# Rest rows masked by the overflow flag, and the last expert's writes behind the overflow branch

## The chip, the cores and the metric

The kernel runs on one core of one Trainium2 chip. The metric is the time of one execution on the device in microseconds (us); the median of three runs is given with the least and the greatest.

## What is computed

An attention layer in chunks of 32 queries (4 batches, 8 heads, 768 positions, 64 wide) gives x, 3072 rows of 512. A mixture of 8 experts follows: each row goes to the two experts with the greatest noisy logits, and the output row is the weighted sum of what they return.

```python
noisy_logits = logits + noise_scale * noise
top2 = np.argpartition(-noisy_logits, 2, axis=1)[:, :2]
top2_l = np.take_along_axis(noisy_logits, top2, axis=1)
top2_l = top2_l - top2_l.max(-1, keepdims=True)
top2_w = np.exp(top2_l)
top2_w /= top2_w.sum(-1, keepdims=True) + 1e-09
out = np.zeros((N, D), dtype=np.float32)
for e in range(E):
    for k in range(2):
        mask = top2[:, k] == e
        h = np.maximum(x[mask] @ w1[e], 0.0)
        out[mask] += top2_w[mask, k, None] * (h @ w2[e])
```

## The kernel before

**Stages.** The attention and the gate come first; their lists of rows are ready some 130 us into the span. The experts follow, one after the other, and fill the rest. The change lies in this second part.

**Rows by pairs of experts.** There are 28 pairs of experts. Each pair has a tile of up to MT = 96 rows that both of its experts work on. Expert e has three pairs for which it is the first (out_of(e)) and three for which it is the second (in_of(e)); four more pairs (numbered from QP = 24) join e and e + 4. Rows of a pair beyond 96 are *rest rows*: up to RU = 64 a pair and RS = 160 an expert are collected in an expert's rest list, in two blocks, A (96 rows) and B (64 rows, written in half rows). If a pair or an expert has still more, the kernel counts that in flag, and a branch at the very end runs overflow(), which works the rows over 96 of every pair off again, in tiles of 128. The flag is copied as a whole number to nxt.

**One expert.** mm1 computes the hidden layer (TensorE, PE), with relu on ScalarE (ACT) and VectorE (DVE). mm2_tiles computes three output tiles. For the first expert of a pair the result is scaled into a new tile y; for the second it is added to that y (line 1063), which is then complete and is noted in the list later. Each PSUM tile holds 32 more rows of another kind, copied to the tile unit: the rest rows of block A (ins_) or the rows of the four pairs from QP (outs). For experts 4 to 7 finish_q scales yq, which holds the other expert's share, and adds unit to it (lines 1085 and 1086); yq goes to later too.

**Writes.** put writes the rows of a y to their places in out, by an indirect DMA that GpSimd (POOL) issues (line 943); places out of bounds are left out. flush issues all that later holds. put_rest (line 960) does the same for a rest tile. A rest row has two experts in different rest lists, so the second expert first reads what the first wrote: get_prev (line 969) reads pA and pB from out after clear_prev has cleared them on ACT (line 1124), and ins_ adds them. Reads of this kind wait for earlier rest writes; writes of y are declared free of both.

**Places of rest rows.** rest_decode (called three times, for experts 0 and 1, 2 and 3, 4 to 7) computes a place from the table entry t: t - 128, or a large number where t is 0, so that unused slots are out of bounds (lines 1250 and 1251).

**Order.** The order on every engine is written out by hand: the loop of lines 1443 to 1482, an iteration an expert. For e below 7 an iteration ends with finish_q, flush, ins_(e). For e = 7 it is: the hidden layer, clear_prev, flush, get_prev, ins_(7), flush, outs(7), finish_q(7). So before the change the three y and the two rest tiles of ins_(7) are written inside the loop, and the three y of outs(7) and the last yq stay in later. A second block then loads nxt on every engine, on DVE behind the last write to yq (last), branches, and flushes (lines 1487 to 1492):

```python
        with tc.issue_after(last[0].ins):
            nov = nc.values_load(nxt[0:1, 0:1], min_val=0, max_val=E * (E + 1),
                                 skip_runtime_bounds_check_because="a count of the counts that are too large")
        with tc.If(nov > 0):
            overflow()
        flush()
```

Line 1518 is the end of the program, where all engines wait for each other.

Of the kernel before, what the change touches and what calls it, by code (L numbers as in the profile page):

```python
# [2 lines left out]

# [8 lines left out]
F32 = mybir.dt.float32  # L12
# [3 lines left out]
Alu = mybir.AluOpType  # L16
# [6 lines left out]
def kernel(  # L23
# [14 lines left out]
    nc = tc.nc  # L38
# [6 lines left out]
    N = B * S  # L45
    Dm = H * D
    E, F = moe_w1.shape[0], moe_w1.shape[2]
# [45 lines left out]
    QP = 3 * E  # L93
    MT = 96
# [3 lines left out]
    BIG = 65536  # L98
# [843 lines left out]
    def put(y, ix, rows=None, n=N):  # L942
        i = nc.gpsimd.indirect_dma_start(  # L943
            out=out if rows is None else rows, out_offset=bass.IndirectOffsetOnAxis(ap=ix, axis=0), in_=y, in_offset=None,
            bounds_check=n - 1, oob_is_err=False)
        for g in ("put", "prev", "rest"):
            tc.declare_no_dep(i.ins, group=g, reason=apart)
        pin(i)
        tc.add_to_no_dep_group("put", i.ins)
# [100 lines left out]
    def mm2_tiles(e, ps, h, unit):  # L1050
        for k, g in enumerate(ps):
            p = psY.tile([128, Dm], F32, name="p_y")
            for f in range(FB):
                nc.tensor.matmul(out=p, lhsT=h[:, f, k, :], rhs=w2(e, f), start=(f == 0), stop=(f == FB - 1))  # L1054
            x = pairs[g].index(e)
            wt = wl[0:MT, x, g:g + 1]
            if x == 0:
                y = ys[g] = yp.tile([128, Dm], F32, name="y")
                nc.scalar.activation(out=y[0:MT], in_=p[0:MT], func=Act.Copy, scale=wt)  # L1059
                keep_unit(0, unit[32 * k:32 * k + 32], p)  # L1060
            else:
                y = ys.pop(g)
                nc.vector.scalar_tensor_tensor(out=y[0:MT], in0=p[0:MT], scalar=wt, in1=y[0:MT], op0=Alu.mult, op1=Alu.add)  # L1063
                keep_unit(1, unit[32 * k:32 * k + 32], p)
                later.append((y[0:MT], dst[0:MT, g:g + 1]))

    def flush():
        for y, ix in later:
            put(y, ix)
        later.clear()  # L1070

    def outs(e):
# [4 lines left out]
        else:  # L1077
            yr_of[e] = unit

    def finish_q(e):  # L1080
        if e >= 4:
            unit = yr_of.pop(e)
            q = QP + e - 4
            y = yq.pop(e - 4)[0:MT]
            nc.vector.tensor_scalar(out=y, in0=y, scalar1=wl[0:MT, 0, q:q + 1], scalar2=None, op0=Alu.mult)
            last[0] = nc.vector.scalar_tensor_tensor(out=y, in0=unit[0:MT], scalar=wl[0:MT, 1, q:q + 1], in1=y, op0=Alu.mult, op1=Alu.add)
            later.append((y, dst[0:MT, q:q + 1]))

    prev = {}
    yr_of = {}  # L1090
# [3 lines left out]
    def ins_(e):  # L1094
        wA, wB, dA, dB, hA, hB_ = rest_of[e]
        pA, pB = prev.pop(e) if e else (None, None)

        def rest_tile():
            p = psY.tile([128, Dm], F32, name="p_y")[:, 0:Dm // 2]
            for f in range(FB):  # L1100
                for g in range(2):
                    nc.tensor.matmul(out=p[g * RU:(g + 1) * RU], lhsT=hB[:, f, :], rhs=w2(e, f, g * Dm // 2, Dm // 2),  # L1102
                                     start=(f == 0), stop=(f == FB - 1), tile_position=(0, g * RU))
            yB = yrp.tile([128, Dm // 2], F32, name="yB", bufs=1)
            if e == 0:
                nc.vector.tensor_scalar(out=yB, in0=p, scalar1=wB, scalar2=None, op0=Alu.mult)
            else:
                nc.vector.scalar_tensor_tensor(out=yB, in0=p, scalar=wB, in1=pB, op0=Alu.mult, op1=Alu.add)  # L1108
            return yB

        unit = yrp.tile([128, Dm], F32, name="yr")
        mm2_tiles(e, in_of(e), hI, unit)
        put_rest(rest_tile(), dB, outB, 2 * N)
        if e == 0:
            nc.vector.tensor_scalar(out=unit[0:MT], in0=unit[0:MT], scalar1=wA, scalar2=None, op0=Alu.mult)
        else:
            nc.vector.scalar_tensor_tensor(out=unit[0:MT], in0=unit[0:MT], scalar=wA, in1=pA[0:MT], op0=Alu.mult, op1=Alu.add)
        put_rest(unit[0:MT], dA, out, N)

    def clear_prev(e):  # L1120
        pA = yrp.tile([128, Dm], F32, name="pA", bufs=1)
# [33 lines left out]
    adr = late.tile([128, 2, E], I32, name="adr")  # L1155
    early = late.tile([128, 2, E], F32, name="early")
    nxt = late.tile([128, 1], I32, name="nxt")
    tsb = late.tile([RU, NP, 8], F32, name="tsb")
    oh_at = scol[0] + 4096
    oh_t = wflat[:, oh_at:oh_at + NG * RU].rearrange("p (g t) -> p g t", g=NG)  # L1160
# [10 lines left out]
    def rest_tables(p, part):  # L1171
        if part == 0:
            pm = p.rearrange("p (a b) -> p a b", a=E)
            nc.vector.tensor_scalar(out=cnt2, in0=pm, scalar1=-float(MT), scalar2=0.0, op0=Alu.add, op1=Alu.max)
            return
        over = late.tile([128, E, E + 1], F32, name="over")
        nc.vector.tensor_scalar(out=over[:, :, 0:E], in0=cnt2, scalar1=float(RU), scalar2=None, op0=Alu.is_gt)
        nc.vector.tensor_scalar(out=cnt2, in0=cnt2, scalar1=float(RU), scalar2=None, op0=Alu.min)
        nc.vector.scalar_tensor_tensor(out=wadr, in0=cnt2, scalar=-float(NP), in1=dadr, op0=Alu.mult, op1=Alu.add)
        cur = cnt2  # L1180
        for i in range(3):
            k = 1 << i
            o = inc2[i % 2]
            nc.vector.tensor_copy(o[:, :, 0:k], cur[:, :, 0:k])
            nc.vector.tensor_tensor(out=o[:, :, k:E], in0=cur[:, :, k:E], in1=cur[:, :, 0:E - k], op=Alu.add)
            cur = o
        ge = late.tile([128, 2, E, E], F32, name="ge")
        for b in range(2):
            nc.vector.tensor_scalar(out=ge[:, b], in0=cur, scalar1=rslot[:, b:b + 1], scalar2=None, op0=Alu.is_le)
        nc.vector.tensor_tensor(out=ge, in0=ge, in1=wadr.unsqueeze(1).to_broadcast([128, 2, E, E]), op=Alu.mult)  # L1190
        red = late.tile([128, 2, E], F32, name="red2")
        nc.vector.tensor_reduce(out=red, in_=ge, axis=AX, op=Alu.add)
        nc.vector.tensor_tensor(out=adr, in0=red, in1=radr, op=Alu.add)
        for b in range(2):
            nc.vector.tensor_scalar(out=early[:, b], in0=cur.rearrange("p a b -> p (a b)")[:, 0:E * E:E + 1],
                                    scalar1=rslot[:, b:b + 1], scalar2=None, op0=Alu.is_gt)
        nc.vector.tensor_scalar(out=over[:, :, E:E + 1], in0=cur[:, :, E - 1:E], scalar1=float(RS), scalar2=None, op0=Alu.is_gt)
        flag = late.tile([128, 1], F32, name="flag")
        nc.vector.tensor_reduce(out=flag, in_=over.rearrange("p a b -> p (a b)"), axis=AX, op=Alu.add)
        nc.vector.tensor_copy(nxt, flag)  # L1200

    def rest_onehots():
        t1 = late.tile([128, NG], F32, name="t1")
# [27 lines left out]
    def rest_decode(lo, hi):  # L1231
# [16 lines left out]
        nc.vector.tensor_tensor(out=w[:, 0], in0=d, in1=w[:, 1], op=Alu.subtract)  # L1248
        nc.scalar.activation(out=w, in_=w, func=Act.Exp)
        nc.vector.tensor_scalar(out=u, in0=t, scalar1=0.0, scalar2=float(BIG), op0=Alu.is_equal, op1=Alu.mult)  # L1250
        nc.vector.scalar_tensor_tensor(out=t, in0=t, scalar=-128.0, in1=u, op0=Alu.add, op1=Alu.max)
        nc.vector.scalar_tensor_tensor(out=t[:, 1], in0=t[:, 1], scalar=2.0, in1=half.to_broadcast([128, m]), op0=Alu.mult, op1=Alu.add)
        nc.vector.tensor_copy(d_, t)
        nc.vector.tensor_scalar(out=u, in0=ea, scalar1=-float(BIG), scalar2=float(BIG), op0=Alu.mult, op1=Alu.add)
# [134 lines left out]
    with tc.manual_schedule(engines={ET.PE, ET.Activation, ET.DVE, ET.SP, ET.Pool}):  # L1389
# [53 lines left out]
        for e in range(1, E):  # L1443
            n = e + 1
            if n == E:
                mm1_rest(e, q=False, engs=(0,))
            mm1_main(e, in_of(e), hI)
            clear_prev(e)
            if e in (1, 3):
                dx = rest_decode(n, 4 if e == 1 else E)  # L1450
                for _ in range(3):
                    next(dx)
            new = gathers(in_of(e + 2)) + gathers(out_of(e + 2)) if e + 2 < E else []
            if e + 2 < 4:
                gather_main(QP + e + 2)
            if n < E:
                rest_rows(n)
            flush()
            get_prev(e)
            load_next()  # L1460
            if n == E:
                ins_(e)
                flush()
            outs(e)
            if n < E:
                turn_rest(n)
            turns(new)
            if e + 2 < E:
                turn_q(e + 2)
            if n < E:  # L1470
                mm1_rest(e, q=False, engs=(0,))
                mm1_main(n, out_of(n), hO)
                mm1_rest(n, r=False)
            finish_q(e)
            if n < E:
                flush()
            if e == 1:
                for k in range(4, E):
                    rest_facts(k)
            load_next()  # L1480
            if n < E:
                ins_(e)
# [40 lines left out]
```

## Time and profile before

| what | us |
|---|---|
| median of 3 runs (least to greatest) | 346.47 (346.16 to 347.88) |
| the profiled execution | 349.4 |
| its span, first to last instruction | 347.8 |
| PE busy in the span | 278.9 (80%) |
| POOL busy in the span | 203.4 (58%) |
| DVE busy in the span | 183.6 (53%) |
| ACT busy in the span | 155.0 (45%) |

Rows of a timeline or a group give the source line, the engine, the operation, the tile written and the tiles read. A name such as POOLq is the sequencer of an engine: it loads registers, branches and handles semaphores, and can be ahead of its engine. "Idle before" with an arrow names what ended the wait. PEclk is the share of TensorE's full clock that was granted. A POOL row of a DMA covers its issue only; the data lands later.

### The profile page before, as it was taken

Reading aid. Unit: us, or ns where it says so; the run is one execution under the profiler, and the core shown is the slowest. Engines: PE = TensorE matmul, PEld = TensorE weight load, DVE = VectorE, ACT = ScalarE, POOL = GpSimd, SP = SyncE. Lnnn points to the kernel's source line nnn. Section 1 sums busy time; section 2 is a strip of 40 time slices with the busy share of each in tenths; the row PEclk is TensorE's granted clock in tenths of the full one; section 3 lists DMA queues with packets and bytes.
Section 4 is the critical chain, followed back from the end, with each engine's and each line's share of the span. In section 5 each row is a group of like instructions: output and inputs, shape, how many; then the busy total and the mean of one; then the engine's idle time right before and its main releaser. Section 6 shows DMA issues by size and latency. Waiting matters only on the chain.

```text
span 347.8 us, 9190 instructions
## 1 busy us (share of the span) xinstructions
PE 278.9 (80%) x3746; PEld 207.2 (60%) x3762; DVE 183.6 (53%) x406; ACT 155.0 (45%) x320; POOL 203.4 (58%) x291
## 2 busy tenths in 40 slices
PE   0678788766777746797999999999999999999800
PEld 0557677655667636656668766676676666866300
DVE  4675568676499677236363533644345354353500
ACT  4657638553565312534445363553443534534200
POOL 4669679982046247745777776571745735626531
PEclk9978899998899556999999999999999999999955
DMA  7999969999516512421686996999999699504221
GB/s 127 211 211 179 224 111 210 192 168 161 106 28 107 140 31 59 109 59 47 114 119 139 160 127 158 185 217 166 186 150 198 159 170 157 152 25 118 79 77 45
DMA packets 43277, 46.78 MB, mean 135 GB/s; under 512 B 20241, under 2 KB 33621, under 8 KB 43228
## 3 DMA queue, kind: packets, MB, share of 16 engines
q0 software_dynamic: 22800, 38.26, 58.8%
q1 hardware_dynamic: 19884, 7.83, 11.6%
q8 instruction: 31, 0.51, 0.6%
q14 instruction: 18, 0.15, 0.1%
q10 hardware_dynamic: 544, 0.03, 0.1%
HBM read 59.11 MB, written 11.33 MB: 203 GB/s over the span
## 4 chain that ended last, share of the span: by engine, by line
PE 44%; issue 6%; DMA 5%; DVE 4%; POOL 2%; ACT 2%; POOLq 1%; DVEq 0%; ACTq 0%
PE p_h L992 23%; PE p_y L1054 17%; DMA pB<-out_dram,ri 4%; POOL out_dram L943 2%; PE p_y L1102 2%; ACT w_all L1149 1%; DMA xt<-xd,main_src 1%; ACT w_all L980 1%; PE p_xt L1214 1%; DVE yq L1048 0%; POOLq L1518 0%; PE p_x L623 0%; POOL out_dram L960 0%; PE p_xt L1148 0%; PE p_list L372 0%
## 5 line engine op out<-in xcount | busy, mean ns | idle before, releaser
L992 PE MATMUL p_h<-w_all 128*128 128x288 bf16 (+3 forms) x1120 | 96.1, 248 | 4.0 <-ACT w_all L1149 2.8
L992 PEld LDWEIGHTS <-w_all 128*128 128x128 bf16 x1120 | 83.1, 99 | 17.7 <-issue 5.9
L1054 PE MATMUL p_y<-w_all 128*128 128x512 bf16 x368 | 83.6, 379 | 1.7 <-ACT yr L1048 0.5
L980 ACT ACTIVATE w_all<-p_h 128x288 bf16<-128x288 f32 (+3 forms) x137 | 46.8, 375 | 51.8 <-PE p_h L992 50.3
L1054 PEld LDWEIGHTS <-w_all 128*128 128x128 bf16 x384 | 37.0, 98 | 43.3 <-issue 1.8
L412 POOL COPY w_all<-w_all 128x512 bf16<-128x512 bf16 (+1 forms) x59 | 42.0, 781 | 13.0 <-PE p_t L432 8.4
L978 DVE TENSOR_SCALAR w_all<-p_h 128x288 bf16<-128x288 f32 (+1 forms) x65 | 30.7, 476 | 35.5 <-PE p_h L992 34.0
L938 POOL DMA_INDIRECT xt<-xd,main_src x28 | 27.0, 963 | 10.1 <-issue 7.3
L1063 DVE SCALAR_TENSOR_TENSOR y<-p_y,main_w,y 96x512 f32<-96x512 f32 x24 | 17.9, 747 | 24.8 <-PE p_y L1054 24.8
L943 POOL DMA_INDIRECT out_dram<-y,main_dst x24 | 22.5, 936 | 12.6 <-issue 6.1
L1048 ACT COPY yr<-p_y 32x512 f32<-32x512 f32 x24 | 13.9, 579 | 35.6 <-DVE y L1063 34.5
L960 POOL DMA_INDIRECT out_dram<-yB,rd x8 | 9.8, 1226 | 28.6 <-DVE yB L1108 28.0
L1059 ACT ACTIVATE y<-p_y,main_w 96x512 f32<-96x512 f32 x24 | 16.4, 682 | 21.2 <-PE p_y L1054 20.1
L432 PE MATMUL p_t<-identf,w_all 128*128 128x128 f32 x120 | 20.6, 314 | 1.3 <-ACT pT L587 0.8
L938 POOL DMA_INDIRECT xt<-xd,rs x16 | 14.8, 924 | 11.3 <-DVE rw L1246 6.3
L1048 DVE COPY yr<-p_y 32x512 f32<-32x512 f32 x12 | 8.3, 694 | 22.3 <-ACT y L1059 21.3
L614 DVE TENSOR_TENSOR w_all<-ps_o,rs 128x512 bf16<-128x512 f32 x24 | 15.7, 683 | 6.5 <-PE ps_o L601 5.6
L1223 POOL DMA_INDIRECT fr<-tdr,adr x16 | 16.1, 1007 | 4.9 <-issue 4.9
L461 PE MATMUL p_v<-identf,w_all 128*128 128x128 f32 x96 | 15.9, 305 | 2.7 <-ACT w_all L436 1.8
L432 PEld LDWEIGHTS p_t<-identf,w_all 128*128 128x128 f32 x120 | 15.9, 163 | 2.7 <-POOL w_all L412 1.4
L587 ACT COPY pT<-p_p 128x1024 bf16<-128x1024 bf16 x11 | 11.1, 1012 | 12.7 <-PE p_p L581 12.4
L501 DVE TENSOR_REDUCE mx<-ps_s 128x16 f32<-128x1024 f32 x12 | 14.7, 1223 | 2.8 <-PE ps_s L488 2.5
(231 smaller groups left out, 405.2 us busy)
## 6 DMA issues: line engine op xcount, KB each, us to landing
w_all<-in_moe_w_dram POOLq DMA_DIRECT2D x16, 1024.0 KB
w_all<-in_k_dram POOLq DMA_DIRECT2D x4, 768.0 KB
w_all<-in_q_dram POOLq DMA_DIRECT2D x4, 768.0 KB
w_all<-in_v_dram POOLq DMA_DIRECT2D x4, 768.0 KB
xd<-w_all SPq DMA_DIRECT2D x24, 128.0 KB
w_all<-mvn SPq DMA_DIRECT2D x24, 32.0 KB
w_all<-xt SPq DMA_TRANSPOSE x39
xt<-xd,main_src POOLq DMA_INDIRECT x28
```

Source lines behind the costliest of these rows:

```text
L412: i = eng.tensor_copy(to, x)
L432: nc.tensor.transpose(out=p_t[:, s, :], in_=m.bitcast(F32)[:, s * 128:(s + 1) * 128], identity=identf)
L938: pin(nc.gpsimd.indirect_dma_start(out=t[0:n].bitcast(I32), out_offset=None, in_=src_, in_offset=bass.IndirectOffsetOnAxis(ap=ix, axis=0)))
L943: i = nc.gpsimd.indirect_dma_start(out=out if rows is None else rows, out_offset=bass.IndirectOffsetOnAxis(ap=ix, axis=0), in_=y, in_offse ...
L978: nc.vector.tensor_scalar(out=out_, in0=in_, scalar1=0.0, scalar2=None, op0=Alu.max)
L980: nc.scalar.activation(out=out_, in_=in_, func=Act.Relu)
L992: nc.tensor.matmul(out=o if len(xk.shape) == 2 else o.rearrange("p (j t) -> p j t", j=xk.shape[1]), lhsT=w_all[:, e % WR, kp * F + f * 128 ...
L1048: (nc.scalar.copy if eng else nc.vector.tensor_copy)(to, p[MT:128, :])
L1054: nc.tensor.matmul(out=p, lhsT=h[:, f, k, :], rhs=w2(e, f), start=(f == 0), stop=(f == FB - 1))
L1059: nc.scalar.activation(out=y[0:MT], in_=p[0:MT], func=Act.Copy, scale=wt)
L1063: nc.vector.scalar_tensor_tensor(out=y[0:MT], in0=p[0:MT], scalar=wt, in1=y[0:MT], op0=Alu.mult, op1=Alu.add)
L1223: i = nc.gpsimd.indirect_dma_start(out=fr[0:n, b, e], out_offset=None, in_=tdr, in_offset=bass.IndirectOffsetOnAxis(ap=adr[0:n, b, e:e + 1 ...
```

## The change

- rest_tables makes a column away = 65536 x flag - 128, and rest_decode uses it in place of the constant -128. With a flag of 0 the places are the same; with a flag above 0 every rest row is out of bounds, and overflow() alone writes rows over 96.
- The puts of expert 7 are all kept in later until behind the branch: three y of ins_, the rest tiles yB and yr, three y of outs, yq. later now holds calls, and the flush behind ins_(7) is gone.
- In ins_(6) a flush stands ahead of the rest tile, so its three y are put ahead of the two rest tiles instead of an iteration later.
- The scaling of yq is taken out of finish_q into scale_q, which stands ahead of outs(e).

```diff
@@ flush, finish_q
-                later.append((y[0:MT], dst[0:MT, g:g + 1]))
+                later.append(partial(put, y[0:MT], dst[0:MT, g:g + 1]))
 
     def flush():
-        for y, ix in later:
-            put(y, ix)
+        for f in later:
+            f()
         later.clear()
...
+    def scale_q(e):
+        if e >= 4:
+            q = QP + e - 4
+            y = yq[e - 4][0:MT]
+            nc.vector.tensor_scalar(out=y, in0=y, scalar1=wl[0:MT, 0, q:q + 1], scalar2=None, op0=Alu.mult)
+
     def finish_q(e):
...
-            nc.vector.tensor_scalar(out=y, in0=y, scalar1=wl[0:MT, 0, q:q + 1], scalar2=None, op0=Alu.mult)
             last[0] = nc.vector.scalar_tensor_tensor(out=y, in0=unit[0:MT], scalar=wl[0:MT, 1, q:q + 1], in1=y, op0=Alu.mult, op1=Alu.add)
-            later.append((y, dst[0:MT, q:q + 1]))
+            later.append(partial(put, y, dst[0:MT, q:q + 1]))
@@ ins_
         mm2_tiles(e, in_of(e), hI, unit)
-        put_rest(rest_tile(), dB, outB, 2 * N)
+        if e == E - 2:
+            flush()
+        yB = rest_tile()
+        later_rest = [partial(put_rest, yB, dB, outB, 2 * N), partial(put_rest, unit[0:MT], dA, out, N)]
+        if e < E - 1:
+            later_rest.pop(0)()
...
-        put_rest(unit[0:MT], dA, out, N)
+        if e < E - 1:
+            later_rest.pop(0)()
+        later.extend(later_rest)
@@ rest_tables, rest_decode
+    away = late.tile([128, 1], F32, name="away")
...
         nc.vector.tensor_copy(nxt, flag)
+        nc.vector.tensor_scalar(out=away, in0=flag, scalar1=float(BIG), scalar2=-128.0, op0=Alu.mult, op1=Alu.add)
...
-        nc.vector.scalar_tensor_tensor(out=t, in0=t, scalar=-128.0, in1=u, op0=Alu.add, op1=Alu.max)
+        nc.vector.scalar_tensor_tensor(out=t, in0=t, scalar=away, in1=u, op0=Alu.add, op1=Alu.max)
@@ the loop
             if n == E:
                 ins_(e)
-                flush()
+            scale_q(e)
             outs(e)
```

More of the change, by code (lines that the diff above doesn't have):

```diff
@@ L1 @@
 import math
+from functools import partial
 from contextlib import ExitStack
```

## The prediction

> **What bounds the kernel now.** I read the page's row of slices first: where does PE stop, and what runs after it?
>
> ```profile
> PE   0678788766777746797999999999999999999800
> POOL 4669679982046247745777776571745735626531
> DMA  7999969999516512421686996999999699504221
> ```
>
> A slice is 347.8 / 40 = 8.7 us. PE is full up to the 37th slice and has nothing in the last two. So there are two stages: a long one that PE sets, and a tail of some 17 us in which POOL (it issues the indirect DMAs that write the output) and the DMA are alone. The change acts mainly on the tail. The timeline of POOL shows its order:
>
> ```profile
> 318.45 0.99 POOL L969 DMA_INDIRECT pA<-out_dram,ri  x1 [0.51 <-ACT pA L1124]
> 319.75 1.03 POOL L969 DMA_INDIRECT pB<-out_dram,ri  x1 [0.30 <-issue]
> ...
> 324.21 1.27 POOL L960 DMA_INDIRECT out_dram<-yB,rd  x1 [3.42 <-DVE yB L1108]
> ...
> 325.78 0.95 POOL L960 DMA_INDIRECT out_dram<-yr,rd  x1 [0.30 <-issue]
> ...
> 327.04 0.92 POOL L943 DMA_INDIRECT out_dram<-y,main_dst  x1 [0.30 <-issue]
> ...
> 328.26 0.92 POOL L943 DMA_INDIRECT out_dram<-y,main_dst  x1 [0.30 <-issue]
> ...
> 329.49 1.00 POOL L943 DMA_INDIRECT out_dram<-y,main_dst  x1 [0.30 <-issue]
> ...
> 335.41 0.92 POOL L943 DMA_INDIRECT out_dram<-y,main_dst  x1 [4.92 <-DVEq L1490]
> ...
> 339.08 0.92 POOL L943 DMA_INDIRECT out_dram<-yq,main_dst  x1 [0.30 <-issue]
> ```
>
> Five puts of expert 7 (yB, yr, three y) are issued by 330.5. POOL then does nothing for 4.92 us, and issues four more from 335.41 to 339.08, (339.08 - 335.41) / 3 = 1.22 us apart. The hole is the overflow branch. The instructions of the branch lines, by the view of one source line (duration least/median/most, then first and last start), say what the hole is made of:
>
> ```profile
> L1488 POOLq TENSOR_LOAD <-nxt x1: 507/507/507, 326.6 to 326.6; - x1
> L1490 POOLq COMPARE_BRANCH  x1: 58/58/58, 327.2 to 327.2; - x1
> L1490 POOLq EVENT_SEMAPHORE  x6: 17/30/43, 329.9 to 332.6; - x6
> L1490 POOLq INC_SWDGE_SEM  x1: 1795/1795/1795, 332.7 to 332.7; - x1
> L1490 PEldq COMPARE_BRANCH  x1: 3782/3782/3782, 328.1 to 328.1; - x1
> L1490 DVEq COMPARE_BRANCH  x1: 72/72/72, 331.6 to 331.6; - x1
> L1490 DVEq EVENT_SEMAPHORE  x1: 21/21/21, 334.5 to 334.5; - x1
> L1518 POOLq DRAIN  x3: 46/109/9904, 337.0 to 347.5; - x3
> ```
>
> POOL's sequencer runs ahead of POOL: it loads the flag at 326.6 and branches at 327.2, before the last three puts have begun. Its next instruction comes at 329.9, 2.6 us on. Six semaphore instructions then spread from 329.9 to 332.6. Then INC_SWDGE_SEM runs 1.80 us, to 334.5, and the first put starts 0.9 us later. What stretches the six? They end 3.2 us after the last put's start (329.49 to 332.7), as they would if the skipped path first lets all earlier POOL transfers land and then adds to their counters what the body would have added. **That is the bound of the tail: puts ahead of the branch must land before the puts behind it may start.** The end follows the last put: 347.8 - 339.08 = 8.7 us, of which POOL's DRAIN (337.0 + 9.9 = 346.9) takes most.
>
> **The change part by part.** *The five puts move behind the branch.* POOL's last work ahead of the branch is now the read of pB. When can the sequencer load the flag? The chain of waits shows it on the next line already while pA is issued:
>
> ```profile
> 318.94 0.02 POOLq L960
> ```
>
> So the load starts at about 318.9 in place of 326.6, the branch is taken at 318.9 + 0.51 + 0.12 = 319.5, and the skipped path is reached 2.6 us later, at 322.1. It has to wait for pB. By the rule read above, 3.2 us after the start of the last transfer, that is 319.75 + 3.2 = 322.95; but the read moves less than a put:
>
> ```profile
> 322.00:324.00 2.00, 1.55 (x19) 0.99 (x18) 1.30 (x3) 0.66 (x2) 0.00 (x0) 1.00 0.00 0
> ```
>
> In this row of the window view (PE, PEld, DVE, ACT and POOL busy; then granted clock, DMA share, GB/s) the DMA is silent from 322.0 on. So pB has moved by 322.0, and six semaphore instructions take some 0.5 us after 322.1. I take INC at 322.7. It ends at 322.7 + 1.8 = 324.5, and the first put starts 0.9 later, at **325.4**.
>
> [...]
>
> The queue behind the branch is then y, y, y, yB, yr, y, y, y, yq. POOL needs 1.22 us a put, 1.57 us for yB (324.21 to 325.78) and 1.26 for yr (325.78 to 327.04). The last put starts at 325.4 + 3 x 1.22 + 1.57 + 1.26 + 3 x 1.22 = **335.6**, against 339.08: **3.5 us earlier**. Is the data there?
>
> ```profile
> 323.85 0.74 DVE L1117 SCALAR_TENSOR_TENSOR yr<-yr,rg,pA 96x512 f32<-96x512 f32 x1
> ...
> 329.24 0.75 DVE L1063 SCALAR_TENSOR_TENSOR y<-p_y,main_w,y 96x512 f32<-96x512 f32 x1 [0.98 <-PE p_y L1054]
> 329.90 0.47 DVE L1085 TENSOR_SCALAR yq<-yq,main_w 96x512 f32<-96x512 f32 x1
> ...
> 330.63 0.75 DVE L1086 SCALAR_TENSOR_TENSOR yq<-yr,main_w,yq 96x512 f32<-96x512 f32 x1 [0.25 <-ACT yr L1048]
> ```
>
> By 324.59 DVE has written the first three y, yB and yr; the last y is written at 329.99 and its put comes at 334.4; yq is written at 331.38 and its put comes at 335.6. Nothing waits for data. POOL's rate is late next, and if all else went, yq could not be put before 331.7.
>
> Bounds of the sum: the branch took POOL 2.6 us, DVE 331.7 to 334.5, 2.8, and PE 3.78 within the instruction, so the first put could be up to 1.1 later. INC has one row; if its 1.8 hide a wait that goes too, the first put could be 1.8 earlier. The other terms repeat within 0.1 us.
>
> *Expert 6: its y puts go ahead of its rest puts.* It counts for pA of expert 7, which reads rows that these rest puts write.
>
> ```profile
> 310.03 0.75 DVE L1063 SCALAR_TENSOR_TENSOR y<-p_y,main_w,y 96x512 f32<-96x512 f32 x1 [0.98 <-PE p_y L1054]
> ...
> 311.79 1.26 POOL L960 DMA_INDIRECT out_dram<-yB,rd  x1 [4.63 <-DVE yB L1108]
> ...
> 313.36 0.92 POOL L960 DMA_INDIRECT out_dram<-yr,rd  x1 [0.30 <-issue]
> ...
> 317.57 0.61 ACT L1124 COPY pA<-zero 128x512 f32<-128x512 f32 x1
> 318.08 0.41 ACT L1124 COPY pB<-zero 128x256 f32<-128x256 f32 x1
> ...
> 323.44 0.48 DVE L1108 SCALAR_TENSOR_TENSOR yB<-p_y,rg,pB 128x256 f32<-128x256 f32 x1 [0.25 <-PE p_y L1102]
> ```
>
> The three y are put in POOL's 4.63 us of idle time; the last is ready at 310.78, is put at 311.1, and so yB comes at 312.3 and yr at 313.9, each 0.5 later. With 3.2 us to land, yr is there at 317.1, but the read of pA waits for ACT's clearing until 318.2 anyway. Hidden, with 1.1 us of cover. If the cover were gone, pB would land later, and behind it stands DVE at 323.44 (released by PE, 1.4 us after the DMA fell silent) before PE itself would be late. I take 0, bounds 0 to 0.5.
>
> *The scale of yq moves ahead of the out tiles.* DVE's 0.47 us (329.90) now falls between 324.6 and the next y. It frees nothing at the end, since yq (330.63) was released by ACT and not by the scale. For experts 4 to 6 it falls into DVE's wait for PE in the same way, and yq is put up to 0.5 us earlier, where POOL has time. I take 0.
>
> *The mask.* The branch is skipped in this trace, so the flag is 0 and the mask changes no address. One more tiny DVE operation writes away, and three decodes take a column as a scalar in place of a constant.
>
> ```profile
> L1195 DVE TENSOR_SCALAR early<-inc,rslot 128x8 f32<-128x8 f32 x2 | 0.4, 273 | 0.0
> ...
> L1218 DVE COPY tsb<-p_xt 64x168 f32<-64x168 f32 x1 | 0.3, 324 | 0.9 <-PE p_xt L1214 0.9
> ...
> L1197 DVE TENSOR_SCALAR over<-inc 128x8 f32<-128x8 f32 x1 | 0.2, 166 | 0.0
> 178.07 0.17 DVE rt L1251
> ```
>
> The new operation (0.17, as L1197) lies ahead of L1218, which waits 0.9 us for PE: nothing while that wait lasts, 0.17 if it goes. A scalar from a column costs by L1195 against L1197, 8 elements each, 0.27 - 0.17 = 0.1 us. The decode is on the chain of waits (the last row is its L1251, start and duration) for experts 2 and 4: 2 x 0.1 = **0.2 us lost**, bounds 0 and 0.3.
>
> *Sum:* -3.5 + 0.2 = -3.3 us. On the profiled execution's own time (349.4, span 347.8) that gives a span of 344.5. The same shift on the median of the runs, 346.47, which is 2.9 us below the profiled execution, gives **343.2 us**, -0.95%.
>
> **The rivals.** *The hole is DVE's, not the landing's.* The profile puts the first put behind the branch down to DVE's own branch event (334.5), not to the landing, and INC ends within some 0.1 us of it. If a put behind the branch must have DVE through it, the first stays at 335.4 and nine queue there: the last starts at 335.4 + 10.2 = 345.6, 6.5 later, 346.47 + 6.5 + 0.2 = 353.2. It decides if no put starts before DVE's event. For it: the releaser in the row. Against: INC starts 1.8 us before that event, right when the semaphore waits end, and a put needs only its own y, which is older.
>
> *The drain counts puts.* DRAIN ends 346.9 - 340.0 = 6.9 us after the last of four puts was issued, and in the last window
>
> ```profile
> 342.00:348.00 6.00, 0.00 (x0) 0.00 (x0) 0.00 (x0) 0.00 (x0) 0.00 (x0) 0.50 0.00 0
> ```
>
> no data moves, so something is worked off. At 6.9 / 4 = 1.7 us a put behind INC, nine cost 8.7 more: 343.2 + 8.7 = 351.9. For it: nothing else explains the silence. Against: data lands at the same pace through the row of puts, so no backlog shows.
>
> *The end does not move.* If the drain ends at a time that the last put does not set, only the 0.2 are left: 346.7. Against: it is POOL's drain and POOL's last work is that put.
>
> *INC was waiting.* If its 1.8 us go, the last put starts at 333.8: 341.4. *The branch is dear* (PE's price): 344.3, in the forecast's range.
>
> **How the numbers follow.** The forecast, 343.2, 342.0 to 344.6 with its bounds, has 0.73. INC's wait 0.07 (341.4), a partial gain in between, to 346, 0.03; the end that does not move 0.06; DVE's hole 0.06; the drain 0.05. A measurement of this kernel tells some 0.5%, 1.7 us, from no change, so faster means under 344.7: 0.73 + 0.07 + 0.02 = 0.82; within, 0.07; slower, 0.11. The range 341.2 to 345.4 holds the first two cases and part of the third, and leaves the last three out.
>
> **What would show it.** Right: POOL's flag load near 319, INC from about 322.7, nine puts in a row from 325.4 to 335.6, no put of expert 7 ahead of the branch, three y puts of expert 6 ahead of its yB, DRAIN ending 6.9 us after the last put is issued. Wrong: a first put after 334.5 (DVE's hole), a silence after the last data well over the present one (the drain), a pA read later than 318.5, or a pause between puts of the row of nine.

## The result and the profile after

| | before | after |
|---|---|---|
| median of 20 runs (lowest to highest) | 348.67 us (346.16 to 351.9) | 345.66 us (342.48 to 348.17) |
| profiled execution, its span | 349.4, 347.8 us | 342.48, 340.9 us |
| mean granted TensorE clock in it | 0.918 | 0.927 |

The ratio of after to before is 0.9916, 95% interval 0.9887 to 0.9945: the kernel is faster by about 0.8%, some 2.9 us. Medians are of all runs, while a ratio, here and below, compares only the runs within 1.5% of the fastest of their kernel (below, that keeps 4 of 6 in e8 and 4 of 8 in e10, and leaves out one run of 690 us each in e1 and e2 and one of before at 436). The forecast was a shift of 3.3 us, 0.95%, which lies in the interval. Its time, 343.2 us, does not hold: the measured 345.66 us lies 0.26 us above the upper end of the range.

The three rows of the page's slices that the prediction began with, now of the changed kernel (a slice is 340.9 / 40 = 8.5 us):

```profile
PE   0666798866987748797999999999999999999910
POOL 4669769974065447726777876471754754734370
DMA  7999979998717502422696996999989689522141
```

There are still two stages. POOL's timeline shows what became of the tail:

```profile
314.45 1.00 POOL L970 DMA_INDIRECT pA<-out_dram,ri  x1 [3.93 <-ACT pA L1137]
315.75 1.03 POOL L970 DMA_INDIRECT pB<-out_dram,ri  x1 [0.30 <-DVE y L1064]
321.71 0.96 POOL L944 DMA_INDIRECT out_dram<-y,main_dst  x1 [4.93 <-DVE yq L1085]
322.97 0.93 POOL L944 DMA_INDIRECT out_dram<-y,main_dst  x1 [0.30 <-issue]
324.21 0.92 POOL L944 DMA_INDIRECT out_dram<-y,main_dst  x1 [0.31 <-issue]
325.43 1.02 POOL L961 DMA_INDIRECT out_dram<-yB,rd  x1 [0.30 <-issue]
326.75 1.42 POOL L961 DMA_INDIRECT out_dram<-yr,rd  x1 [0.30 <-issue]
328.48 0.92 POOL L944 DMA_INDIRECT out_dram<-y,main_dst  x1 [0.30 <-issue]
...
332.15 0.92 POOL L944 DMA_INDIRECT out_dram<-yq,main_dst  x1 [0.30 <-issue]
```

The hole of 4.9 us is still there, but it has moved ahead of all nine puts. It now lies, from 316.78 to 321.71, while PE computes. The branch lines, by the view of one source line:

```profile
L1505 POOLq COMPARE_BRANCH  x1: 58/58/58, 315.4 to 315.4; - x1
L1505 POOLq EVENT_SEMAPHORE  x6: 17/30/43, 318.6 to 319.0; - x6
L1505 POOLq INC_SWDGE_SEM  x1: 1695/1695/1695, 319.1 to 319.1; - x1
L1505 DVEq EVENT_SEMAPHORE  x1: 21/21/21, 330.6 to 330.6; - x1
L1533 POOLq DRAIN  x3: 46/109/12600, 327.4 to 340.6; - x3
```

Absolute times of two executions can't be compared, since the same code ahead of the tail takes different times (below). So I cut each execution in four: the *head* up to the first gather of an expert's rows, the *middle* up to the end of the last matmul, the *tail* up to the start of the last put, and the rest. The cuts of before, from its timelines of POOL and PE (a matmul missing from the count does not move the end):

```profile
130.44 1.05 POOL L938 DMA_INDIRECT xt<-xd,main_src  x1 [1.89 <-DVE d_last L336]
...
323.86 5.34 PE L1054 MATMUL p_y<-w_all 128*128 128x512 bf16 x23 [0.45 <-ACT yr L1048]
```

and of after:

```profile
126.10 1.05 POOL L939 DMA_INDIRECT xt<-xd,main_src  x1 [1.88 <-DVE d_last L337]
...
319.86 5.34 PE L1055 MATMUL p_y<-w_all 128*128 128x512 bf16 x24 [0.45 <-ACT yr L1049]
```

| us | head | middle | tail | rest |
|---|---|---|---|---|
| before | 130.44 | 198.75 | 339.08 - 329.20 = 9.88 | 8.71 |
| after | 126.10 | 199.09 | 332.15 - 325.20 = 6.95 | 8.72 |

The two profiled executions differ by 6.9 us of span. The tail gives 2.9 of it, nearly the 3.0 by which the medians differ. The middle loses 0.3. The head gives 4.3, and in the head the change touches nothing.

### The profile page after: what moved, and what is told of

Same layout as the page of the kernel before. It is cut to its first block, busy times and chain, and to the rows that moved or that the text cites. A ratio compares the mean times of both kernels' runs of the same rounds, so it can differ in the third digit from the quotient of the medians.

```text
span 340.9 us, 9211 instructions
## 1 busy us (share of the span) xinstructions
PE 278.6 (82%) x3762; PEld 206.3 (61%) x3762; DVE 183.7 (54%) x407; ACT 155.0 (45%) x320; POOL 203.2 (60%) x291
## 4 chain that ended last, share of the span: by engine, by line
PE 51%; DVE 4%; issue 3%; DMA 2%; ACT 2%; POOL 2%; POOLq 0%; DVEq 0%; ACTq 0%
PE p_h L993 27%; PE p_y L1055 20%; PE p_y L1108 2%; DMA pB<-out_dram,ri 1%; POOL out_dram L944 1%; ACT w_all L1162 1%; DMA xt<-xd,main_src 1%; ACT w_all L981 1%; POOL out_dram L961 1%; PE p_xt L1229 1%; DVE yq L1049 0%; POOLq L1533 0%; PE p_x L624 0%; PE p_xt L1161 0%; PE p_list L373 0%
## 5 line engine op out<-in xcount | busy, mean ns | idle before, releaser
L1055 PE MATMUL p_y<-w_all 128*128 128x512 bf16 x384 | 85.9, 379 | 1.1 <-DVE yq L1049 0.7
L433 PE MATMUL p_t<-identf,w_all 128*128 128x128 f32 x120 | 18.5, 290 | 1.2 <-DVE kT L437 0.5
L462 PE MATMUL p_v<-identf,w_all 128*128 128x128 f32 x96 | 16.6, 314 | 2.8 <-ACT w_all L437 1.9
L502 DVE TENSOR_REDUCE mx<-ps_s 128x16 f32<-128x1024 f32 x12 | 14.7, 1222 | 2.9 <-PE ps_s L489 2.6
L437 ACT COPY w_all<-p_v 128x512 f32<-128x512 f32 x21 | 12.0, 588 | 7.7 <-PE p_v L462 7.6
```

Of the source, the lines that this page charges most:

```text
L433: nc.tensor.transpose(out=p_t[:, s, :], in_=m.bitcast(F32)[:, s * 128:(s + 1) * 128], identity=identf)
L462: nc.tensor.transpose(out=p_v[:, i, c, :], in_=vT[:, c, c0:c0 + 128], identity=identf)
```

## The experiments

Two theories were carried in. **L**, the prediction's: puts ahead of the overflow branch must land, and POOL's skipped path must run, before a put behind it starts; so the tail is set by the last POOL DMA ahead of the branch and by the queue behind it. **P**: a put that meets a DVE operation with two inputs in SBUF is stretched, and that is why one put of after took 1.42 us. A third, **R**, says that the tail varies from execution to execution as the head does; e0 was run for it. The rivals on record (the hole is DVE's, the drain counts puts, the end does not move, INC was waiting) were read from the same runs. All edits are to the changed kernel unless "to before" is said.

### The changed kernel once more

No edit.

> The changed kernel itself, for a time and a profile beside the others. Terms: tail = start of the last put minus end of the last matmul (9.88 us before, 6.95 us after the change in the two profiles there are); middle = first gather of rows to last matmul (198.75 and 199.09); head = span start to first gather (130.44 and 126.10). Theory L (puts ahead of the branch had to land before those behind it): tail 6.9 to 7.0 again, ratio to before about 0.992. Theory R (the tail shifts from run to run as the head does): tail anywhere between 6.9 and 9.9.

345.38 us, ratio 0.9885 (0.9832 to 0.9939). Tail 6.43, rest 8.72. The tail is half a microsecond below the 6.9 to 7.0 expected; one put makes the difference (0.93 us here, 1.42 in after), and the last section says why. But the span is 344.1 and not 340.9: the head took 129.99 us. That is the first sign that the level of one profile says little.

### The order kept, the branch where it was

```diff
-        if e < E - 1:
-            later_rest.pop(0)()
+        later_rest.pop(0)()
...
-        if e < E - 1:
-            later_rest.pop(0)()
-        later.extend(later_rest)
+        later_rest.pop(0)()
...
                 ins_(e)
+                flush()
```

> The changed kernel with the five puts of expert 7 ahead of the branch and in the order of the kernel before: yB, yr, y, y, y, so that three y that are ready wait in POOL's queue behind yB. Theory L (the first put behind the branch starts some 5.7 to 5.9 us after the last POOL transfer ahead of it was issued): the last put ahead is late again, 0.3 us after the last matmul began its end, tail 9.8 to 10.0 us, ratio to before 0.998 to 1.002. If something else in the change (mask, scale, expert 6's order) gave the gain: tail 6.4 to 7.0.

348.79 us, ratio 1.0018 (0.9986 to 1.005), tail 9.98: with yB, yr, y, y, y ahead of the branch all the gain is gone, and the mask, the scale and expert 6's order, which this kernel keeps, show nothing that can be measured. Its POOL timeline around the hole:

```profile
322.82 1.27 POOL L961 DMA_INDIRECT out_dram<-yB,rd  x1 [3.43 <-DVE yB L1114]
...
328.10 0.91 POOL L944 DMA_INDIRECT out_dram<-y,main_dst  x1 [0.30 <-issue]
334.12 0.91 POOL L944 DMA_INDIRECT out_dram<-y,main_dst  x1 [5.11 <-DMA pA<-out_dram,ri]
```

The first put behind the branch comes 6.02 us after the last one ahead of it. The profile names three different releasers for this hole: DVE's branch event in before, DVE's yq in after, a DMA of pA here. None of them is the cause, and the distance stays.

### Five puts ahead of the branch again, but y first

```diff
                 ins_(e)
+                flush()
```

> The changed kernel with the flush behind ins_(7) put back, so that yB, yr and three y are put ahead of the branch again; mask, scale and expert 6's order stay changed. Theory L: POOL's semaphore instructions spread again over some 3 us until the fifth put has landed, the tail is 9.7 to 10.0 us, the ratio to before 0.999 to 1.002. Theory R: tail as in the changed kernel or anywhere. If the scale or expert 6's order gave the gain: tail 6.9 to 7.0.

This missed. I had expected the tail of before, since five puts are ahead of the branch again. It was 6.37 us, and the time 346.08 us, ratio 0.9926 (0.9886 to 0.9965). The order is what I had overlooked: the three y now come ahead of yB, and POOL can put them while yB is not yet computed.

### To before, the order alone

```diff
         mm2_tiles(e, in_of(e), hI, unit)
+        if e == E - 1:
+            flush()
         put_rest(rest_tile(), dB, outB, 2 * N)
```

> The kernel before with one line alone: in expert 7 the three y are put ahead of the rest tiles, all five still ahead of the branch. Theory L: the last put ahead of the branch is issued 3.0 us before the last matmul ends, as in the kernel with the flush put back, the tail is 6.3 to 6.5 us and the ratio to before 0.990 to 0.995: the order alone is worth as much as the move behind the branch. Rival (the move behind the branch is what counts): tail 9.9, ratio 1.0.

346.91 us, ratio 0.9878 (0.9821 to 0.9935), tail 6.35. In the tail, one inserted flush gives what the whole change gives, with the branch where it was; the time, from few runs, fits that and shows no more. Its POOL timeline:

```profile
320.43 1.03 POOL L969 DMA_INDIRECT pB<-out_dram,ri  x1 [0.30 <-issue]
321.77 0.96 POOL L943 DMA_INDIRECT out_dram<-y,main_dst  x1 [0.30 <-issue]
...
325.50 1.01 POOL L960 DMA_INDIRECT out_dram<-yB,rd  x1 [0.30 <-DVE yr L1119]
326.82 0.93 POOL L960 DMA_INDIRECT out_dram<-yr,rd  x1 [0.30 <-issue]
332.56 0.92 POOL L943 DMA_INDIRECT out_dram<-y,main_dst  x1 [4.81 <-DVE yq L1086]
```

Before's first put row says the same from the other side: yB waits 3.42 us for DVE, and the three y behind it in POOL's order are all finished by 323.20, before yB is:

```profile
322.45 0.75 DVE L1063 SCALAR_TENSOR_TENSOR y<-p_y,main_w,y 96x512 f32<-96x512 f32 x1 [0.98 <-PE p_y L1054]
323.44 0.48 DVE L1108 SCALAR_TENSOR_TENSOR yB<-p_y,rg,pB 128x256 f32<-128x256 f32 x1 [0.25 <-PE p_y L1102]
```

With y first, that wait is filled, the last put ahead of the branch is issued 3.06 us before the last matmul ends instead of 0.29 after it, and the hole shifts with it.

### To before, the late puts alone

The three y of expert 7, then yB and yr, are put behind the branch; mask, scale and expert 6 stay as before.

```diff
...
-        put_rest(rest_tile(), dB, outB, 2 * N)
+        yB = rest_tile()
+        if e < E - 1:
+            put_rest(yB, dB, outB, 2 * N)
...
+        if e < E - 1:
+            put_rest(unit[0:MT], dA, out, N)
+        else:
+            late_rest.append((yB, dB, outB, 2 * N))
+            late_rest.append((unit[0:MT], dA, out, N))
...
-                flush()
...
+        for a in later[:3]:
+            put(*a)
+        del later[:3]
+        for a in late_rest:
+            put_rest(*a)
```

> The kernel before with one part of the change alone: the five puts of expert 7 behind the branch, in the changed kernel's order; no mask, no moved scale, expert 6 as before. The rest rows' places are not masked when the overflow branch is taken, which it is not here. Theory L: the whole gain, tail 6.9 to 7.1 us, middle 198.5 to 198.9 (without the mask's 0.2), ratio to before 0.990 to 0.993. If the other parts carry it: tail 9.9.

345.87 us, ratio 0.9906 (0.9862 to 0.9949), tail 6.95 as in after (and as there one put, yr's, is stretched, to 1.37 us). The read of pB starts 9.44 us before the last matmul ends, as in after (9.44) and e0 (9.45), though here expert 6 still puts its rest rows first. So expert 6's order is worth nothing for the tail, as the prediction had it. The middle, expected below before's, was 199.79: spreads of 1 us in it are not the mask's.

### pA and pB cleared earlier

ACT clears pA and pB ahead of expert 7's hidden rest layer, so that their reads, and with them the branch, can come earlier.

```diff
+                clear_prev(e)
                 mm1_rest(e, q=False, engs=(0,))
...
-            clear_prev(e)
+            if n < E:
+                clear_prev(e)
```

> The changed kernel with the clearing of pA and pB for expert 7 moved ahead of its hidden layer, so that their read no longer waits for ACT but for expert 6's rest rows to land. Theory L (what POOL does ahead of the branch must have landed): pA is read 1.9 us earlier against the last matmul, the first put behind the branch and the last one follow by 1.9, tail 5.0 to 5.2 us, ratio to before 0.985 to 0.988. Rival (the branch or DVE's data set the first put): tail stays 6.9. Rival (ACT is late with the relus of the hidden layer): the middle grows by 0.5 to 1 us.

345.37 us, ratio 0.9889 (0.9835 to 0.9943). The tail fell to 4.64, and pB starts 11.23 us before the last matmul ends, 1.8 earlier. (The 5.0 to 5.2 expected was reckoned from the 6.95 of after; 1.8 off the 6.43 of e0 is 4.6.) But the clearing makes ACT late for the hidden layer, and PE waits for it in mid-stage; ACT's and PE's timeline:

```profile
314.59 0.62 ACT L1137 COPY pA<-zero 128x512 f32<-128x512 f32 x1 [0.82 <-DVE yr L1128]
...
316.08 4.08 PE L993 MATMUL p_h<-w_all 128*128 128x288 bf16 x32 [0.39 <-ACT w_all L981]
```

What the tail gained beyond after, no time shows; the middle came out at 199.75, and of that only the 0.39 are traced.

### The clearing on POOL

```diff
-            nc.scalar.copy(to, zero.to_broadcast(list(to.shape)))
+            if e == E - 1:
+                nc.gpsimd.memset(to, 0.0)
+            else:
+                nc.scalar.copy(to, zero.to_broadcast(list(to.shape)))
```

> The changed kernel with expert 7's pA and pB cleared by POOL itself (in its idle time while expert 6's rest rows land) and not by ACT. Theory L: pA is read as soon as the rest rows have landed, some 1.8 us earlier against the last matmul, tail 4.5 to 5.1 us, and without the 0.4 us of idle PE that the early clearing on ACT cost; ratio to before 0.982 to 0.988. Rival (POOL's clearing takes longer than its idle time): tail 5.5 to 7.0.

345.13 us, ratio 0.9871 (0.9831 to 0.991), tail 6.17 and not the 4.5 to 5.1 expected. pB is earlier by 1.2 us, but the skipped path is reached later. By the view of the branch line:

```profile
L1508 POOLq COMPARE_BRANCH  x1: 58/58/58, 318.3 to 318.3; - x1
L1508 POOLq EVENT_SEMAPHORE  x6: 17/30/43, 322.0 to 322.4; - x6
L1508 POOLq INC_SWDGE_SEM  x1: 1695/1695/1695, 322.5 to 322.5; - x1
```

From the end of the branch to the first semaphore it took 3.66 us, 3.06 in after. That is 0.6 of the 0.9 us by which the first put is late; the other 0.3 is the branch itself, which POOL takes as pB starts (318.26) and not 0.3 before. Was the 3.66 chance? The same kernel once more:

> The kernel in which POOL clears expert 7's pA and pB, a second time: its branch took 3.66 us to reach the skipped path in the first profile, against 3.02 to 3.08 in the four other kernels with nine puts behind the branch. If that was chance: 3.0 to 3.1, first put 5.9 us after pB's read, tail 5.1 to 5.4 us. If it belongs to where the branch now falls: 3.6 to 3.7 and tail 6.1 to 6.3 again.

346.96 us, ratio 0.9866 (0.9802 to 0.9931); 3.56 us again, tail 6.09. The six other profiles with nine puts behind the branch have 3.02 to 3.25 (the two highest in e6 and e5 below). So this price belongs to this program and not to one execution. The traces show one more thing: the DMA queue that brings instructions. In the window from the end of the branch to the first semaphore, of after and then of e9 (queue and kind: packets, MB, share of 16 engines):

```profile
q14 instruction: 1, 0.01, 0.6%
```

```profile
q14 instruction: 2, 0.02, 1.6%
```

On this queue it is two in e9 and e10, and one in each of the eleven other profiles. Where it is one, the packet starts 0.9 to 1.6 us after the branch, and the skipped path begins 1.6 to 1.8 us after the packet starts. So the price goes with a second packet of instructions. The queue does not name the engine that it serves, so that the packets are POOL's is inferred from these times; why this program has two stays open. Neither of these versions can be told from the changed kernel in time.

### Mask alone, expert 6 alone, DVE work beside the puts

These three ran once each, on a chip on which the granted clock was 0.84 to 0.85 and before took 434.38 us. Only distances within the tail are compared.

To before, the mask alone (away's operation and the decode's column): 

> The kernel before with the mask alone (one more tiny DVE operation, and the column away as a scalar in the three decodes). My term: the decode operation takes 0.27 in place of 0.17 us three times, twice on the chain, so the middle (first gather to last matmul, 198.75 before) grows by 0.2 us; the tail stays 9.9. Rival: the column costs nothing, middle unchanged within 0.1.

433.97 us, tail 9.93, first put behind the branch 5.95 after the last ahead of it: the mask changes nothing there.

Expert 6's y put behind its rest rows again:

```diff
-        if e == E - 2:
-            flush()
```

> The changed kernel without the flush ahead of expert 6's rest rows: its three y are put behind them, as before the change. By the prediction this edit is hidden under ACT's clearing of pA: tail 6.9 to 7.0 us as in the changed kernel. Rival (the edit is part of the gain): pA is read later than the end of the clearing and the tail grows by up to 1 us.

429.46 us. The tail is 7.39 us, more than the 6.9 to 7.0 expected, since pB is read 0.7 us nearer to the end of the last matmul than in the next run (-8.74 against -9.45). The rival forecast that size, but its reason doesn't show: pA is read at 401.70, released by ACT's clearing, 7.2 us after expert 6's last rest put (394.49). The clearing itself ends nearer to the last matmul, 10.0 us ahead of it and 10.7 in the next run; PE has done four of the first 23 output matmuls ahead of a wait for ACT here, and none there. Whether the order of expert 6 has a part in that stays open on this chip: mask alone, with the order of before, has pB at -8.81, but e2, also with it and at the usual clock (mean 0.924; 0.843 here), at -9.44. The first put comes 6.15 us after pB, as with y first on this chip (6.11, next run).

Six more DVE operations with two inputs in SBUF, of no use to the output, behind the last yq:

```diff
+            if e == E - 1:
+                spare = wflat[:, 3 * WE + 2 * Dm:3 * WE + 4 * Dm].bitcast(F32)
+                for _ in range(6):
+                    nc.vector.scalar_tensor_tensor(out=spare[0:MT], in0=unit[0:MT], scalar=wl[0:MT, 1, q:q + 1], in1=y, op0=Alu.mult, op1=Alu.add)
```

> The changed kernel with six more DVE operations that read two SBUF tiles (the form of the last write to yq, 0.75 us each, into a buffer that nothing reads), in a row behind that write and so beside the last puts. Theory P (a DVE operation with two SBUF inputs holds up the issue of a put): the three or four puts beside them take 1.2 to 1.5 us in place of 0.92, and the tail grows by 0.8 to 2. Rival (yr's 1.42 us after the change and yB's 1.27 before have another cause): those puts stay at 0.92, the tail at 6.9 to 7.0.

431.59 us, tail 6.96. Only two puts came to lie beside the six, since DVE waited 2.86 us for its own branch first; one of them was stretched. P's three or four did not come, nor its longer tail, but the rows say when a put takes longer. DVE and POOL, from the timeline:

```profile
415.46 0.75 DVE L1092 SCALAR_TENSOR_TENSOR yq<-yr,main_w,yq 96x512 f32<-96x512 f32 x1 [0.64 <-ACT yr L1049]
415.73 1.28 POOL L961 DMA_INDIRECT out_dram<-yr,rd  x1 [0.30 <-issue]
...
419.07 4.67 DVE L1097 SCALAR_TENSOR_TENSOR w_all<-yr,main_w,yq 96x512 f32<-96x512 f32 x6 [2.86 <-DVEq L1509]
419.77 0.92 POOL L944 DMA_INDIRECT out_dram<-y,main_dst  x1 [0.30 <-issue]
420.99 1.18 POOL L944 DMA_INDIRECT out_dram<-yq,main_dst  x1 [0.30 <-issue]
```

The put at 415.73 starts 0.48 us before the operation of 415.46 ends (416.21) and takes 0.35 more than the 0.93 it has in e0. The six operations are 4.67 / 6 = 0.78 apart if evenly spaced, so the first ends at 419.82 and the put of 419.77 has 0.05 of it left: no stretch. The third ends near 421.39, 0.40 after the put of 420.99 starts: 0.26 more than 0.92. These two puts, which start within such an operation, thus take longer by what is left of it, less some 0.13 (0.48 - 0.35, 0.40 - 0.26).

## Why the prediction was right in size and wrong in level

**The bound: right, but only half of it decides after the change.** From the start of the last POOL DMA ahead of the branch to the first put behind it, in every profile but the three of the slower chip (us; "semaphores" is from the first of the six to the end of the last):

| kernel | last POOL DMA ahead of the branch, start against the end of the last matmul | from branch to skipped path | semaphores | INC | first put behind, after that DMA's start | first to last put behind |
|---|---|---|---|---|---|---|
| before | last y, +0.29 | 2.61 | 2.78 | 1.80 | 5.92 | 3.67 (4 puts) |
| e7, order kept | last y, +0.30 | 2.98 | 2.83 | 1.80 | 6.02 | 3.66 (4) |
| e8, order alone | yr, -3.06 | 2.78 | 1.06 | 1.80 | 5.74 | 3.67 (4) |
| e1, y first, ahead | yr, -3.02 | 2.56 | 1.28 | 1.80 | 5.73 | 3.67 (4) |
| after | pB, -9.44 | 3.06 | 0.45 | 1.70 | 5.96 | 10.44 (9) |
| e0, after again | pB, -9.45 | 3.02 | 0.46 | 1.70 | 5.93 | 9.95 (9) |
| e2, late puts alone | pB, -9.44 | 3.08 | 0.46 | 1.70 | 5.98 | 10.41 (9) |
| e4, early clearing | pB, -11.23 | 3.02 | 0.45 | 1.70 | 5.94 | 9.94 (9) |
| e9, POOL clears | pB, -10.65 | 3.66 | 0.46 | 1.70 | 6.88 | 9.94 (9) |
| e10, e9 again | pB, -10.64 | 3.56 | 0.46 | 1.70 | 6.79 | 9.94 (9) |

The first numbers plus the last two of a row give the tail: for after -9.44 + 5.96 + 10.44 = 6.96. The distance stays at 5.7 to 6.0 us wherever the branch falls, but for the program of e9.

It is made of different parts, though. With puts ahead (first four rows) the six semaphores spread over 1 to 3 us: POOL waits there for landings. In before the last packet of POOL's DMA queue ends at 332.0 and the fourth semaphore comes at 332.46; in e7, e8 and e1 it is 0.36 to 0.43 us from the one to the other. With only reads ahead (other rows) the six come within 0.46 us and nothing waits: after's DMA is silent by 318.0 us,

```profile
318.00:319.00 1.00, 1.00 (x14) 0.66 (x14) 0.55 (x1) 0.08 (x1) 0.00 (x0) 1.00 0.00 0
```

and the skipped path begins only at 318.6. There the way through the branch decides, 0.3 us ahead of pB and 3 us long, as the prediction had worked it out. Nothing in these runs makes the two sums equal: that both come to nearly 6 us looks like chance, and e9, where the way is longer, breaks it.

**The rivals: refuted.** DVE's hole: after's first put starts at 321.71, DVE's branch event comes at 330.6. The drain counts puts: DRAIN ends 327.4 + 12.6 = 340.0, 6.9 us after the last put's issue ended (333.07), with nine puts as with four. INC was waiting: 1.70 to 1.80 us in all kernels, with a landing to wait for or without; what it does in that time, no trace shows. The end does not move: the rest is 8.71 to 8.72 us in all these kernels, wherever the last put starts.

**The steps, by size.** First put: 5.96 us after pB's start instead of 5.65. The skipped path was reached 3.06 us after the branch instead of 2.6, and that price was in my bounds (PE's 3.78). The branch itself takes 58 ns and POOL's next instruction comes 2.6 to 3.7 us later (third column); the packets of instructions shown under e9 fall into that time. Whether POOL waits for them, no run shows. Queue of nine: 9.95 in e0 instead of 10.15, since yB took 1.02 and not 1.27; 10.44 in after, since yr took 1.42. That is more than the 0.1 us within which the prediction let such terms repeat. Last put against the end of the last matmul, predicted 3.5 earlier: 2.9 in after, 3.45 in e0.

**The mask: a tenth of a microsecond.** The decode by the view of its line, in before and in after:

```profile
L1251 DVE SCALAR_TENSOR_TENSOR rt<-rt,ru x3: 163/164/166, 159.0 to 224.2; 128x4 f32<-128x4 f32 x2, 128x8 f32<-128x8 f32 x1
```

```profile
L1266 DVE SCALAR_TENSOR_TENSOR rt<-rt,away,ru x3: 222/223/225, 154.8 to 220.1; 128x4 f32<-128x4 f32 x2, 128x8 f32<-128x8 f32 x1
```

0.223 - 0.164 = 0.06 us each, not 0.1; for two on the chain 0.12 instead of 0.2. Scale and expert 6: nothing that shows at the usual clock, as predicted (e7, e2); e5, on the slower chip, leaves expert 6 open.

**Missed, though it does not change the sum.** I put the gain down to moving puts behind the branch. The change does a second thing that is enough alone: it takes the three y out from behind yB. e8 and e1 show it. That both ways give nearly the same tail (6.35 and 6.43) follows from their sums and from nothing deeper: e8 has the branch later by -3.06 + 9.45 = 6.4 us and 9.95 - 3.67 = 6.3 less to issue behind it. The prediction quoted the 3.42 us wait of yB and the three y behind it, and did not ask what that wait costs.

**The step that failed** is "The same shift on the median of the runs, 346.47". Three runs of before gave 346.47; the median of 20 is 348.67, 2.2 us more. On that base the same 3.3 us give 345.4, 0.3 from the measured 345.66; and the measured shift of 3.0 on the old base would have given 343.5, well inside the range. So the base alone took the time out of it. The profiled execution's own 349.4 us was the warning: I noted that it lay 2.9 us above the median and gave the level no width of its own in the range, which held only the bounds of the mechanism.

## To carry to other kernels

When an engine that issues in order (here POOL with its puts: before's three y, finished by 323.20, are put from 327.04 on, behind yB at 324.21) waits for the data of one row, look for finished work that stands behind that row before moving anything across a branch; a line that reorders may do as much as a restructuring. A branch that POOL's DMAs have to cross cost nearly the same distance after the last DMA ahead of it in eleven profiles (5.7 to 6.2 us; 6.8 to 6.9 in the two of e9's program), so put it where another engine covers that, and read a hole by such distances in several kernels, not by the releaser that one row names. And give the base its own width: three runs of a kernel whose runs spread over 1.6% do not fix its median to 0.5%.

## What was not expected of the hardware

**A put's issue takes up to 0.5 us longer when it starts within a DVE operation with two inputs in SBUF.** Beside e6's rows: after's put at 326.75 starts 0.62 us before L1092 (326.62, 0.75 long) ends and takes 1.42 instead of 0.93, 0.49 more. Before's yB at 324.21 starts 0.38 before L1117 (323.85, 0.74) ends and takes 1.27 instead of 1.02, 0.25 more. Again it is what is left, less 0.13. e2's yr, at 330.90 with 0.57 left, takes 1.37, 0.44 more. In all thirteen profiles 67 puts start within such an operation at least 0.1 us behind its start and with 0.3 or more of it left; each takes 1.18 to 1.42 us, and of the 505 other puts none takes more than 1.06. One of these starts within an operation that has an input in PSUM: before's put at 329.49, with 0.50 left of L1063 (329.24, 0.75), takes 1.00. In e0 the two start together, and it is DVE that takes a little longer, 0.80 us where after has 0.75:

```profile
330.40 0.80 DVE L1092 SCALAR_TENSOR_TENSOR yq<-yr,main_w,yq 96x512 f32<-96x512 f32 x1 [0.65 <-ACT yr L1049]
...
330.48 0.93 POOL L961 DMA_INDIRECT out_dram<-yr,rd  x1 [0.30 <-issue]
```

The 0.49 is nearly all of the difference between the tails of after and e0 (6.95 and 6.43). By what the one holds up the other, no run here shows.

**The same head takes 126 to 132 us.** In the ten profiles of the eight kernels timed here the head runs from 126.10 to 132.38 us, with the same code on the same data. Between after and e0, 3.9 us of head outweigh everything the change is worth. They arise in one place, between the ninth and the tenth reduction of the attention (L502). The windows from 82 us on, of after and then of e0 (columns as in the prediction):

```profile
82.00:92.00 10.00, 9.69 (x226) 8.68 (x220) 8.22 (x13) 6.73 (x12) 0.00 (x0) 0.83 0.95 155
```

```profile
82.00:95.00 13.00, 10.37 (x212) 9.72 (x204) 7.11 (x12) 6.07 (x12) 0.00 (x0) 0.74 0.71 119
```

The ninth reduction starts at 83.77 in after and at 83.48 in e0, the tenth at 90.82 and at 94.58. In e0 the granted clock of the stretch is 0.74 instead of 0.83, and PE also stands idle there for 2.6 us (its waits ahead of L602's ps_o) for nothing that the profile shows. Whether the clock or that idle time comes first, the traces don't tell, and no run here set out to.
